# Loading queries and keys two tokens per lane: 512-byte runs, and the even and odd tokens of a tile kept apart

## The chip, the cores and the metric

The kernel runs on one core of a Trainium2 chip. The core has a matrix engine (PE, with its own weight loads, PEld), a vector engine (DVE), a scalar engine for activations (ACT), a general engine (POOL), and SP, which in this kernel only issues transfers. Sixteen DMA engines carry the transfers. The engines run apart from each other and meet at semaphores. The metric is the time of one execution on the device in microseconds (us), as a median of several; lower is better.

## The reference

Two layers are computed, one after the other. The first is attention with 4 batches, 8 heads, 768 tokens and 64 numbers per head. Each token sees the first 8 tokens ("global") and the 96 tokens up to itself ("local"), with a bias that falls linearly with distance:

```python
scores = scale * q @ k^T                                  # per batch and head
rel = pos[:, None] - pos[None, :]
is_global = pos[None, :] < 8
is_local = (rel >= 0) & (rel < 96)
dist = where(is_global & ~is_local, 96.0, abs(rel))
scores = where(is_global | is_local, scores - slope[h] * dist, -1e9)
x = softmax(scores) @ v                                   # heads side by side: 4 x 768 x 512
```

The global rule holds with no regard to order, so a token among the first 8 sees the others of the 8 that come after it.

The second layer is a mixture of 4 attention experts over `x`, each with a head of 64 numbers and causal, and the best 2 of 4 weighted by a gate:

```python
logits = x @ w_gate; the two largest per token, softmax over the two
for e in range(4):
    ye = softmax(causal(scale * (x @ wq[e]) @ (x @ wk[e])^T)) @ (x @ wv[e]) @ wo[e]
    out += weight_of_e_per_token * ye                     # out: 4 x 768 x 512
```

Inputs and output are float32. The kernel works in float16 between them and accumulates in float32.

## The kernel before, in words

**Units.** The work is cut into 24 units `u`: 4 batches times 6 tiles of 128 tokens (`ri` is the tile's number in its batch, `P` = 128). `unit(u)` writes down all operations of one unit. A unit has a front (the first layer) and a back (the second layer).

**Front.** Three loads (`ldq`, `ldk`, `ldv`, L519) bring 128 tokens of all 8 heads into `raw`, one token per lane, so that a lane receives 8 runs of 256 bytes (one head's 64 float32). POOL casts them to float16 (`cq`, `ck` into `qk16`, `cv` into `V1`). PE transposes queries and keys of a pair of heads at a time (`tq`, L536, 8 transposes per unit into one PSUM tile), and DVE copies the result to `qkT` (`eq`). PE makes the scores transposed, keys on lanes and queries along the row (`s0`, `s1`, L559: tile `sc`, one half of the heads each, with the tile's own keys and those of the tile before it). ACT takes the exponential (`x0`, `x1`, L563), DVE multiplies by a precomputed factor `M` that holds both bias and mask (`m0`, `m1`, L568; `M0` in the first tile of a batch), PE multiplies with the values (`z0`, `z1`, L576 and L579), whose column of ones gives the softmax sum, and DVE divides (`r0`, `n0` and so on, L590 and L592) into `x16`.

**Global tokens.** The 8 global keys and values of a batch are saved from its tile 0 (`kg`, `vg`, into `KG` and `VG`). When tile `u` has been used as own tile, they are written over the first 8 keys and values of it (`kp` on POOL, `vp` by a DMA on SP, L600), so that the next tile, which reads tile `u` as the tile before, meets the global tokens there. With a reach of 96 those 8 places are not otherwise seen by it.

**Back.** PE transposes `x16` (`tx`, L608), taking every fourth column so that the contraction index matches the weights' layout; DVE copies to `xT` (`ex`). PE projects to the queries and keys of the four experts (`pq`, L618, 16 matmuls) and to values and gate logits (`pv`, L624); the first is copied to `QK2` (`eqk`), the second to `V2` (`ev`). Scores of the second layer go against all earlier tiles of the batch (`s2`, L658), ACT takes exponentials (`x2`, L662), POOL clears the part above the diagonal (`af`, L670), PE multiplies with the values (`y2`, L682, up to 24 matmuls), DVE weights the result (`rz`, `cw`, `n2`), PE transposes (`tz`, L700) and projects (`po`, L705), ACT copies to `o_sb` (`eo`) and SP stores it (`so`, L714; 128 runs of 2 KB).

**Order of the work.** Every engine executes its instructions in the order in which the program gives them. That order is made while the program is built, by a small planner, `Stream`. Every operation is entered with the engines that may do it and an assumed length, with the operations it must follow, and with a rank. `Stream.run` repeatedly takes the operation with the earliest possible start by the assumed lengths (the key is start + `OTHER` if the second of two allowed engines does it + `ALPHA` * rank) and emits it. So the order is fixed on every engine, and the choice of engine for operations that have two (`eqk`, `ev`, `eo`, `m0`, `m1`, `kg`, `kp`) is made there too. SP is a queue like the others: a transfer that waits holds back all that come after it in the list. The program also has each transfer wait until the one eight places earlier in SP's list has landed, so that at most eight are under way.

**Buffers.** `R` = 4: `raw`, `qkT`, `V1` and most others are rings of four tiles, `qk16` of three. PSUM has two slots for scores (`s`) and four for the rest (`w`).

A `general_path` at the end is taken only if sums leave a safe range; it doesn't run here. One helper, `copy` (L358), does all casts and copies, so these are told apart by their tiles.

Of the kernel before, what the change touches and what calls it, by code (L numbers as in the profile page):

```python
# [16 lines left out]
P = 128  # L17
# [4 lines left out]
PACE, ALPHA, TURN = 6.00622, 0.000375979, 0.1  # L22
OTHER = {"m0": 3.12, "m1": 3.35, "eqk": 1.71, "ev": 14.02, "eo": 5.29, "kg": -15.22, "kp": 7.23}
RANK = {
    "ldq": 3.09, "ldk": -1.4103, "ldv": 10.549, "cq": 15.151, "ck": -10.082, "cv": -4.5336,
    "tq": -71.653, "eq": 55.538, "kg": 47.24, "vg": 107.76, "kp": -9.0259, "vp": -19.463,
    "s0": -7.8612, "s1": -17.799, "x0": -50.605, "x1": -67.881, "m0": 14.187, "m1": 99.879,
    "z0": -20.335, "z1": -37.532, "r0": -131.8, "r1": -26.257, "n0": 17.285, "n1": 25.757,
    "tx": -57.992, "ex": 9.4907, "pq": -14.609, "eqk": -26.055, "pv": 28.034, "ev": 73.988,
    "xr": 65.128, "mx": 2.1683, "wr": 21.14, "zi": 51.323, "s2": 11.269, "s2+": 19.618,  # L30
    "x2": 60.753, "x2+": 71.931, "af": -92.082, "y2": 41.953, "rz": 30.062, "cw": 42.106,
    "n2": -35.324, "tz": -7.6056, "ez": -136.19, "po": 59.119, "eo": 47.072, "so": -50.942,
}
W_RANK = -47.481, 2.337, 16.829, -53.198, 17.758
# [287 lines left out]
def kernel(  # L322
# [40 lines left out]
    R = 4  # L363
    ident = const.tile([P, P], FH, name="ident")
    w32 = const.tile([P, 3, E, nko, Hd], F32, name="w32")
# [6 lines left out]
    d = const.tile([P, 2 * P], F32, name="d")  # L372
    dg = const.tile([P, P], F32, name="dg")
# [6 lines left out]
    KG = ring(2, [P, H // 2, N_G], FH, "KG")  # L380
    VG = ring(2, [N_G, H, DV + 1], FH, "VG")
    raw = ring(R, [P, 3, H, Dh], F32, "raw")
    qk16 = ring(3, [P, 2, H, Dh], FH, "qk16")
    qkT = ring(R, [P, 2, H // 2, P], FH, "qkT")
# [22 lines left out]

    def c_iota(e):

        for n in range(2):  # L410
            pool.iota(di[:, n * P:(n + 1) * P], pattern=[[1, P]], channel_multiplier=-1, base=n * P)

    def c_mask(e):
        pool.affine_select(out=d[:, 0:P], in_=d[:, 0:P], pattern=[[1, P]], channel_multiplier=-1,
                           base=0, compare_op=Alu.is_ge, fill=HUGE)
        for n in range(2):
            t = d[:, n * P:(n + 1) * P]
            pool.affine_select(out=t, in_=t, pattern=[[-1, P]], channel_multiplier=1,
                               base=N_L - 1 - n * P, compare_op=Alu.is_ge, fill=HUGE)

    def c_dg(e):

        pool.memset(dg[:, :], float(N_L))
        pool.affine_select(out=dg[:, :], in_=dg[:, :], pattern=[[0, P]], channel_multiplier=-1,
                           base=N_G - 1, compare_op=Alu.is_ge, fill=HUGE)
# [21 lines left out]
    st.add("mask", c_mask, {"POOL": 0.9}, ["d"], rank=-18.0)  # L447
# [48 lines left out]
    def unit(u):  # L496
# [21 lines left out]
        def load(n, src):  # L518
            return lambda e: nc.sync.dma_start(raw[i][:, n, :, :],  # L519
                                               src[b, :, rows, :].rearrange("h s d -> s h d"))  # L520

        for n, src in enumerate((q, k, v)):
            add("ld" + "qkv"[n], load(n, src), {"DMA": 1.2}, [("c" + "qkv"[n], u - R)])
        for n in range(2):
            add("c" + "qk"[n], lambda e, n=n: copy(e, qk16[u % 3][:, n, :, :], raw[i][:, n, :, :]),
                {"POOL": 0.53} if u else ({"POOL": 0.53}, {"DVE": 0.4})[n],
                ["ld" + "qk"[n], ("tq", u - 3)])
# [266 lines left out]
```

## Time and profile before

| | |
|---|---|
| median of 3 runs | 158.49 us (158.09 to 159.02) |
| the profiled execution's own time | 157.58 us |
| its span, first to last instruction | 155.8 us |
| TensorE clock granted, mean over the span | 0.983 (1.00 until 148 us) |
| busy PE, DVE, ACT, POOL | 124.4, 126.7, 111.0, 72.0 us |
| first and last PE instruction | start at 10.44, end at 149.15 us |
| last ACT copy of the output | start at 149.23 us, 0.58 us |
| read from and written to HBM | 20.98 MB and 6.29 MB |

The profile tells of one execution. Busy time is the time in which an engine has an instruction in flight; PE's matmuls are pipelined, so one 128x128 matmul lasts 0.22 us by itself but 16 of `pq` in a row take about 0.9 to 1.0 us. A row of groups gives the line, the engine, the operation, the tiles (out<-in), the shapes and the count, then busy us and mean ns of one, then the idle time just before such instructions and what ended it. A row of waits gives who waited for whom: us in total, times, longest. A row of windows gives, for a stretch of time, the busy us of each engine (and the count of its instructions), the granted clock, the time of all transfer packets as a share of the 16 DMA engines' time (packets overlap, so it can exceed 1) and GB/s.

### The profile page before, as it was taken

What the parts mean: (1) busy time and instruction counts of PE and PEld (TensorE: products, weight loads), DVE (VectorE), ACT (ScalarE), POOL (GpSimd) and SP (SyncE); (2) the same over time, 40 slices, a digit from 0 to 9 for tenths busy, and PEclk for the clock granted to TensorE, in tenths of its full rate; (3) what the DMA queues carried; (4) which work ended last, traced back from release to release, by engine and by line L of the source; (5) the groups of instructions that cost most, each with busy time, mean ns of one, the idle gap of its engine ahead of it and who ended that gap; (6) DMA issues with size and microseconds to landing.
All of it is one profiled execution on the core that took longest, in us unless ns stands there. A gap on an engine that the chain in (4) does not pass through costs nothing.

```text
span 155.8 us, 5666 instructions
## 1 busy us (share of the span) xinstructions
PE 124.4 (80%) x2246; PEld 99.6 (64%) x2246; DVE 126.7 (81%) x438; ACT 111.0 (71%) x186; POOL 72.0 (46%) x132
## 2 busy tenths in 40 slices
PE   0027885959888988998899989999699999999820
PEld 0015774737777767985777876867588788777400
DVE  3228678987999999898899999999699999978710
ACT  4902457646867987889499968996478879999810
POOL 5037433636476655557938465654392321221000
PEclk9999999999999999999999999999999999999985
DMA  2999669899997999998997999995990221232550
GB/s 52 315 222 215 180 201 231 166 203 234 222 215 137 207 251 217 212 199 172 260 230 206 224 232 199 265 210 144 221 186 4 76 76 67 74 135 74 196 208 13
DMA packets 80687, 27.85 MB, mean 179 GB/s; under 512 B 75632, under 2 KB 77328, under 8 KB 80656
## 3 DMA queue, kind: packets, MB, share of 16 engines
q1 hardware_dynamic: 80656, 27.45, 77.7%
q8 instruction: 18, 0.29, 0.9%
q14 instruction: 13, 0.11, 0.3%
HBM read 20.98 MB, written 6.29 MB: 175 GB/s over the span
## 4 chain that ended last, share of the span: by engine, by line
PE 35%; DVE 21%; DMA 20%; POOL 6%; ACT 5%; issue 5%; SPq 4%; POOLq 0%; ACTq 0%; DVEq 0%
DMA raw<-in_q_dram 13%; DMA raw<-in_k_dram 7%; PE pq L618 6%; DVE A L568 5%; POOL qk L358 5%; PE tq L536 5%; PE po L705 4%; PE z L682 4%; PE s L658 4%; DVE qkT L358 4%; PE pv L624 3%; ACT A L563 3%; PE sc L559 3%; DVE QK L358 2%; DVE cw L689 2%
## 5 line engine op out<-in xcount | busy, mean ns | idle before, releaser
L563 ACT ACTIVATE A<-sc 128x1024 f16<-128x1024 f32 (+1 forms) x48 | 44.8, 962 | 16.0 <-PE sc L559 15.8
L662 ACT ACTIVATE A<-s 128x1024 f16<-128x1024 f32 (+1 forms) x48 | 44.0, 929 | 9.1 <-PE s L658 9.0
L358 POOL CAST qk<-raw 128x512 f16<-128x512 f32 x47 | 31.4, 671 | 31.2 <-DMA raw<-in_q_dram 19.2
L568 DVE TENSOR_TENSOR A<-A,M 128x1024 f16<-128x1024 f16 (+1 forms) x48 | 32.8, 690 | 1.6 <-ACT A L563 1.4
L536 PE MATMUL tq<-ident,qk 128*128 128x128 f16 x192 | 16.1, 231 | 16.3 <-POOL qk L358 15.8
L618 PE MATMUL pq<-xT,wqk 128*128 128x128 f16 x384 | 26.2, 223 | 0.9 <-DVE xT L358 0.7
L670 POOL TENSOR_SCALAR_AFFINE_SELECT A<-A 128x512 f16<-128x512 f16 x24 | 16.8, 699 | 18.8 <-ACT A L662 17.7
L618 PEld LDWEIGHTS <-wqk 128*128 128x128 f16 x384 | 23.1, 100 | 2.6 <-issue 0.9
L536 PEld LDWEIGHTS <-qk 128*128 128x128 f16 x192 | 12.2, 103 | 19.3 <-POOL qk L358 18.1
L358 POOL CAST V<-raw 128x512 f16<-128x512 f32 x24 | 16.2, 675 | 12.2 <-DMA raw<-in_v_dram 6.8
L358 DVE COPY qkT<-tq 128x1024 f16<-128x1024 f16 x24 | 16.3, 678 | 4.1 <-PE tq L536 3.9
L576 PE MATMUL z<-V,A 128*128 128x65 f16 x192 | 17.7, 198 | 2.3 <-POOL V L358 0.9
L592 DVE TENSOR_TENSOR x<-z,rall 128x256 f16<-128x256 f32 x48 | 19.2, 412 | 0.0
L358 DVE CAST QK<-pq 128x512 f16<-128x512 f32 x24 | 16.3, 680 | 1.6 <-PE pq L618 1.6
L658 PE MATMUL s<-QK 64*128 64x128 f16 x336 | 16.2, 218 | 1.3 <-DVE QK L358 1.1
L559 PE MATMUL sc<-qkT 64*128 64x128 f16 x192 | 15.2, 226 | 1.9 <-DVE qkT L358 1.0
L576 PEld LDWEIGHTS <-A 128*128 128x128 f16 x192 | 13.7, 100 | 3.8 <-DVE A L568 1.2
L358 ACT COPY o_sb<-po 128x512 f32<-128x512 f32 x24 | 14.4, 606 | 2.2 <-PE po L705 1.3
L579 PE MATMUL z<-V,A 128*128 128x65 f16 x160 | 14.9, 195 | 0.1
L624 PE MATMUL pv<-wvg,xT 128*128 128x264 f16 x96 | 14.8, 276 | 0.0
L559 PEld LDWEIGHTS <-qkT 64*128 64x128 f16 x352 | 10.9, 97 | 5.9 <-issue 2.8
L705 PE MATMUL po<-wo,zT 128*128 128x512 f16 x48 | 14.3, 380 | 0.3 <-DVE zT L358 0.2
(57 smaller groups left out, 197.9 us busy)
## 6 DMA issues: line engine op xcount, KB each, us to landing
raw<-in_k_dram SPq DMA_DIRECT2D x24, 256.0 KB
raw<-in_q_dram SPq DMA_DIRECT2D x24, 256.0 KB
raw<-in_v_dram SPq DMA_DIRECT2D x24, 256.0 KB
out_dram<-o_sb SPq DMA_DIRECT2D x24, 256.0 KB
w<-in_moe_wq_dram SPq DMA_DIRECT2D x1, 512.0 KB
w<-in_moe_wk_dram SPq DMA_DIRECT2D x1, 512.0 KB
w<-in_moe_wv_dram SPq DMA_DIRECT2D x1, 512.0 KB
wo<-in_moe_wo_dram SPq DMA_DIRECT2D x1, 512.0 KB
```

Of the source, the lines that this page charges most:

```text
L358: act.copy(o, i) if e == "ACT" else (dve if e == "DVE" else pool).tensor_copy(o, i)
L536: nc.tensor.transpose(ps[:, s, p, :], qk16[u % 3][:, s, 2 * p:2 * p + 2, :], ident[:, :])
L559: mm(sc[:, par, pr, prev * P:(prev + 1) * P], lhsT=kt, rhs=qkT[i][L, 0, p, :], start=True, stop=True)
L563: act.activation(A1[(2 * u + hf) % (2 * R)][:, :, :, 0:w], T.pop(("s", u, hf))[:, :, :, 0:w], func=Exp, scale=scale1)
L568: eng[e].tensor_tensor(a, a, M[:, hf, :, :, :] if ri else M0[:, hf, :, :, :], op=Alu.mult)
L576: mm(z[:, h % 4, :], lhsT=a[:, par, pr, 0:P], rhs=V1[i][:, h, 0:DV], start=True, stop=not ri)
L592: add(f"n{hf}", lambda e, hf=hf, r1=r1: dve.tensor_tensor(x16[i][:, 256 * hf:256 * hf + 256].rearrange("p (h d) -> p h d", d=Dh), T.pop((" ...
L618: mm(ps[:, j, :], lhsT=wqk[:, ko, j, :], rhs=xT[i][:, ko, :], start=(ko == 0), stop=(ko == nko - 1))
L624: mm(ps[:, :], lhsT=xT[i][:, ko, :], rhs=wvg[:, ko, :], start=(ko == 0), stop=(ko == nko - 1))
L658: mm(sc[:, par, n, :], lhsT=QK2[b % 2][L, ki, 2 + p2, :], rhs=QK2[b % 2][L, ri, p2, :], start=True, stop=True)
L662: act.activation(A2[i][:, :, 4 * ch:4 * ch + m, :], T.pop(("s2", u, ch))[:, :, 0:m, :], func=Exp, scale=scale2)
L705: mm(ps[:, :], lhsT=zT[i][:, p2, :], rhs=wo[:, p2, :], start=(p2 == 0), stop=(p2 == E // 2 - 1))
```

## The change

Queries and keys are loaded, cast and transposed in blocks of two tiles. In a block of 256 tokens lane `p` receives tokens `2p` and `2p+1`, which lie side by side in HBM, so a run is 512 bytes. The cast sorts a lane's two tokens apart (`p h j d -> p j h d`), the transposes are done for even tokens (`j` = 0) and odd tokens (`j` = 1) separately, and so within each tile of 128 the tokens stand as 64 even ones followed by 64 odd ones. The values are loaded in the same order, with two transfers of 64 lanes each (still runs of 256 bytes). The order is undone where `x` is transposed anyway: the transpose multiplies with a permuted identity, `perm`. The mask factors and the 8 global tokens (now 4 even and 4 odd ones, so two pieces of 4 lanes) follow the new order. The planner's constants, ranks and some assumed lengths are new as well; which engine does an operation, and its place in the order, follow from them.

```diff
-PACE, ALPHA, TURN = 6.00622, 0.000375979, 0.1
-OTHER = {"m0": 3.12, "m1": 3.35, "eqk": 1.71, "ev": 14.02, "eo": 5.29, "kg": -15.22, "kp": 7.23}
+PACE, ALPHA, TURN = 8.35723, 4.54359e-06, 0.1
+OTHER = {"m0": 8.31, "m1": 7.38, "eqk": -0.06, "ev": 16.85, "eo": 9.76, "kg": -28.92, "kp": 23.68}
 RANK = {
...
-W_RANK = -47.481, 2.337, 16.829, -53.198, 17.758
+W_RANK = -104.69, -69.793, 42.697, 5.1292, 57.145
...
-    raw = ring(R, [P, 3, H, Dh], F32, "raw")
-    qk16 = ring(3, [P, 2, H, Dh], FH, "qk16")
-    qkT = ring(R, [P, 2, H // 2, P], FH, "qkT")
+    RB = 3
+    rawqk = ring(RB, [P, 2, H, 2, Dh], F32, "rawqk")
+    rawv = ring(R, [P, H, Dh], F32, "rawv")
+    qk16 = ring(RB, [P, 2, 2, H, Dh], FH, "qk16")
+    qkT = ring(RB, [P, 2, H // 2, 2, P], FH, "qkT")
...
+    def c_perm(e):
+        pool.tensor_copy(perm[:, :].rearrange("c (p j) -> c p j", j=2),
+                         ident[:, :].rearrange("c (j p) -> c p j", j=2))
...
     def c_mask(e):
-        pool.affine_select(out=d[:, 0:P], in_=d[:, 0:P], pattern=[[1, P]], channel_multiplier=-1,
-                           base=0, compare_op=Alu.is_ge, fill=HUGE)
...
+        for op, lim in ((Alu.is_lt, 0.0), (Alu.is_gt, N_L - 0.5)):
+            dve.tensor_scalar(dout[:, :], d[:, :], lim, HUGE, op0=op, op1=Alu.mult)
+            dve.tensor_tensor(d[:, :], d[:, :], dout[:, :], op=Alu.max)
...
-        for n, src in enumerate((q, k, v)):
-            add("ld" + "qkv"[n], load(n, src), {"DMA": 1.2}, [("c" + "qkv"[n], u - R)])
-        for n in range(2):
-            add("c" + "qk"[n], lambda e, n=n: copy(e, qk16[u % 3][:, n, :, :], raw[i][:, n, :, :]),
...
+        u0, bl = u - u % 2, u // 2
+        if u == u0:
+            for n, src in enumerate((q, k)):
+                x = "qk"[n]
+                r, h16, tb = rawqk[bl % RB], qk16[bl % RB], qkT[bl % RB]
+                add("ld" + x, lambda e, r=r, n=n, src=src: nc.sync.dma_start(
+                    r[:, n, :, :, :].rearrange("p h j d -> p h (j d)"),
+                    src[b, :, ri * P:(ri + 2) * P, :].rearrange("h (p j) d -> p h (j d)", j=2)),
+                    {"DMA": 1.85}, [("c" + x, u - 2 * RB)])
+                add("c" + x, lambda e, r=r, h16=h16, n=n: copy(
+                    e, h16[:, n, :, :, :], r[:, n, :, :, :].rearrange("p h j d -> p j h d")),
+                    {"POOL": 1.05} if u else ({"ACT": 0.95}, {"DVE": 0.6})[n],
+                    ["ld" + x, ("t" + x, u - 2 * RB)])
+                def tq(e, n=n, x=x, h16=h16):
+                    T["t" + x, u] = ps = wtile([P, H // 2, 2, 2, HP], FH, "t" + x)
+                    for p in range(H // 2):
+                        for j in range(2):
+                            nc.tensor.transpose(ps[:, p, :, j, :], h16[:, n, j, 2 * p:2 * p + 2, :], ident[:, :])
...
+        def load_v(e):
+            for j in range(2):
+                nc.sync.dma_start(rawv[i][j * HP:(j + 1) * HP, :, :],
+                                  v[b, :, rows, :].rearrange("h (p j) d -> j p h d", j=2)[j])
...
-            add("vp", lambda e: nc.sync.dma_start(V1[i][0:N_G, :, :], VG[b % 2][:, :, :]), {"DMA": 0.1},
+            def vp(e):
+                for j in range(2):
+                    L = slice(j * HP, j * HP + NG2)
+                    nc.sync.dma_start(V1[i][L, :, :], VG[b % 2][L, :, :])
...
-                nc.tensor.transpose(ps[:, ko, :], xv[:, ko, :], ident[:, :])
+                nc.tensor.transpose(ps[:, ko, :], xv[:, ko, :], perm[:, :])
```

## The prediction, made before the changed kernel was run

> **What bounds the kernel now.** I read the busy row first, then the windows, then the groups and waits of the engine that is fullest where it matters, and the transfers last.
>
> ```profile
> PE 124.4 (80%) x2246; PEld 99.6 (64%) x2246; DVE 126.7 (81%) x438; ACT 111.0 (71%) x186; POOL 72.0 (46%) x132
> ...
> DMA  2999669899997999998997999995990221232550
> q1 hardware_dynamic: 80656, 27.45, 77.7%
> ```
>
> Over the whole span nobody is full. By stage it differs; the columns below are the stretch and its length, then busy us (instructions) of PE, PEld, DVE, ACT, POOL, the clock, DMA share, GB/s:
>
> ```profile
> 12.00:36.00 24.00, 18.54 (x276) 15.09 (x276) 19.21 (x58) 12.89 (x20) 12.12 (x22) 1.00 0.90 201
> 36.00:116.00 80.00, 72.63 (x1384) 59.19 (x1382) 74.88 (x247) 63.19 (x98) 49.18 (x85) 1.00 1.00 213
> 116.00:148.00 32.00, 31.25 (x574) 24.20 (x572) 28.45 (x118) 28.87 (x51) 7.11 (x13) 1.00 0.25 87
> 120.00:136.00 16.00, 15.87 (x322) 12.77 (x321) 15.10 (x58) 13.89 (x25) 3.51 (x7) 1.00 0.20 71
> ```
>
> Until 116 us, while inputs are loaded, the DMA engines are full (share 1.00) at only 213 GB/s, DVE is at 94% and PE at 91%. After the loads PE is at 98%. So two things hold up the first stage, transfers and DVE, and in the last nothing is left but PE's own work.
>
> I keep the books by PE, because it works from 10.44 to 149.15 us and the end follows it by a fixed tail (one copy, one store: 6.65 us). Of these 138.7 us it is busy 124.4, so 14.3 us are lost. The waits say to whom (who waited for whom: us in total, times, longest):
>
> ```profile
> POOL qk L358 <- DMA raw<-in_q_dram: 19.2, 16, 6.5
> ...
> PE tq L536 <- POOL qk L358: 15.8, 10, 10.4
> ...
> PE s L658 <- DVE QK L358: 1.1, 1, 1.1
> ...
> PE sc L559 <- DVE qkT L358: 1.0, 2, 0.8
> ```
>
> The first PE wait includes the start (10.4), so 15.8 - 10.4 = 5.4 us inside the run are waits for casts that themselves waited for transfers. The other 14.3 - 5.4 = 8.9 us are many small waits; those that the table of groups gives to DVE (before `pq` 0.7, `z` 0.7 and 0.5, `sc` 1.0 and 0.4, `s` 1.1, `tx` 0.6, `tz` 0.6, `tq` 0.3 and 0.2, `po` 0.2) add up to 6.3.
>
> **Part 1: loads of queries and keys.** 48 transfers of 1,024 packets of 256 bytes become 24 of 1,024 packets of 512 bytes: 49,152 packets become 24,576. In the trace's packet records a 256-byte packet lasts 20.4 ns (mean of 73,728), one of 1,024 bytes 53.9 and one of 2,048 bytes 94.9. No 512-byte packet is there. Bounds: 20.4 (size costs nothing) and 40.8 (no better than two). I take the straight line between the 256 and 1,024 rows, 20.4 + 33.5/3 = 31.6. Then 49,152 x 20.4 = 1,003 us of engine time become 777, so 226/16 = 14 us are saved (0 to 31) of the 77.7% x 155.8 = 121 us that all queue packets take. Share 1.00 in the load stage falls to about 0.87. The Trainium skill (DMA: Bandwidth & Descriptors, Specifications) puts the least size for line rate at 512 bytes, with read-modify-write below it. By that rule the 512-byte packet would run at the rate of the 2,048-byte rows, an estimate of 94.9/4 = 23.7 ns and a saving of 26 us. Both leave the transfers off the limit.
>
> Rings also get deeper: three blocks are six tiles, before four tiles raw and three cast. I therefore take the 5.4 us of PE waits as gone: **-5.4** (0 to -5.4). What is late next is POOL: a cast of a block has 1,024 numbers per lane, between 0.61 (median of the 512 row) and twice that, and delivers two tiles at once. 22 of these replace 47, so POOL's sum does not grow.
>
> **Part 2: values and global tokens.** 24 value loads become 48 of 64 lanes with the same packets; 20 `vp` copies of 8 lanes become 40 of 4. SP issues 24 fewer loads of q and k, 24 more of v and 20 more `vp`. A `vp` issue takes 0.65 us (median), so SP gets 20 x 0.65 = 13 us more issue work in 155, mostly in time in which it stood waiting for `o_sb` (22.9 us in one row of its waits) or for `z`. At most eight transfers are under way, and 6 instead of 5 per unit must pass: 8 places then cover 1.33 units instead of 1.6, about 8 us at 6 us per unit, against a landing time of 4 to 6.7 us on the chain. Behind a `vp` that waits for its `z` stand the loads of the following blocks. I cost it at nothing inside the run; the cover is the deeper ring, and without it a late load costs what it did before (part 1's 0). A rule speaks against it: SBUF — State Buffer ("Can I just issue two DMAs to hit both halves?") of the Trainium skill says 64 lanes reach half of the 16 ports, 196 GB/s measured, and that two halves do not add up. By that rule a tile's values take an estimated 262 KB/196 GB/s = 1.34 us, 24 of them 2.6 us more than at the 213 GB/s of the windows, still within the 14 saved. Four more `vg` copies of about 0.69 us go to POOL, which is idle half the time.
>
> **Part 3: which engine copies QK.** The built order shows what the diff alone does not: with the new constants 16 of the 24 `eqk` copies go from DVE to ACT. From the groups:
>
> ```profile
> L358 DVE CAST QK<-pq 128x512 f16<-128x512 f32 x24 | 16.3, 680 | 1.6 <-PE pq L618 1.6
> ...
> L358 ACT COPY o_sb<-po 128x512 f32<-128x512 f32 x24 | 14.4, 606 | 2.2 <-PE po L705 1.3
> ```
>
> DVE loses 16 x 0.68 = 10.9 us, ACT gains 16 x 0.606 = 9.7 (the same shape of copy). DVE comes to 126.7 - 10.9 + 1.7 (mask, below) + 0.3 (the first block's cast) = 117.8, ACT to 111.0 + 9.7 + 1.1 (first block's cast of q, like the 128x1024 weight cast, 1.07) = 121.8; PE stays at 124.4, as its 2,246 matmuls keep their shapes. All three are then about equal, and DVE has 9 us of slack it lacked. Of the 6.3 us that PE loses to DVE I take half: **-3.2** (0 to -6.3; 0 if ACT's queue delays the copies as much as DVE's did).
>
> **Part 4: the start.** Three POOL selects (0.29 + 0.55 us) become four DVE operations on 128x256 float32. The rows nearest are 0.29 (cast 128x256) and 0.32 (128x128, two inputs), so 1.2 to 2.1 us, 1.7 taken. That delays ACT's 16 factor exponentials (3.40 to 7.55 us) by about a microsecond, still before the first cast that ACT does. SP's new list begins wq, wk, q0, k0, each 512 KB, where before half of q0 and k0 sufficed. From 4 us on at the 312 GB/s of 4 to 8 us, k0 (2.1 MB, of which 0.24 by 4 us) lands at about 10; before, q0 landed at 9.72. So first scores come at 12.5 to 13 instead of 12.26. The first values stand tenth, behind 3.7 MB: 15 to 20 us at 312 to 213 GB/s, against a cast at 13.39 before. `z` of unit 0 (14.28 before) comes that late; PE, DVE and ACT have the fronts of units 1 to 3 to do meanwhile, which the new order places there. **+1.0** (0 to +4).
>
> **Part 5: the end.** Before, after the last `pq` (139.28) PE has 7.6 us of work from several units until the last `y2` ends (146.87). In the new order only `po`, `y2` of unit 22, 24 `s2`, `tz`, `po` and 24 `y2` remain: 0.43 + 0.60 + 0.83 + 0.25 + 0.43 + 0.91 = 3.5 us. Unit 23's three exponentials of 1.03 us stand between its `s2` and `y2` with only 0.7 us of other work for PE, and the PSUM ring for scores has two places, so the third group waits for the first exponential. PE idles about **+1.6** (0 to +2.5).
>
> The remaining edits (ring shapes, `perm` in place of `ident`, transposes writing two runs of 64, 4-lane `kg`/`kp` pieces) issue as many instructions of the same size as before on PE, DVE and POOL: 0; the `perm` copy, once on POOL before 10 us, is covered by POOL's idle 6.5 us there.
>
> **Sum.** -5.4 - 3.2 + 1.0 + 1.6 = -6.0 us. The profiled execution took 157.58 (span 155.8 and 1.8 around it), so 151.6; the median shown lies 0.9 above that execution, which would make 152.5. I say 152.0.
>
> **Rivals.**
>
> 1. *The transfers stay the limit.* If a 512-byte packet costs about 40 ns, or the eight places bind, part 1 gives 0 and the time is 152.0 + 5.4 = 157.4. For it: the share of 1.00 and landing times over 4 us. Against: 355 GB/s worth of rate at 2 KB (71 GB/s at share 0.20).
> 2. *Slower: ACT becomes the bound, in its queue.* QK copies on ACT stand behind exponentials of 1.03 us, and `s2` of the unit and all later tiles of the batch wait for them. From 12 to 148 us ACT was busy 105.0 of 136 (77%); with 10.8 more it has 115.8. If it again reaches only the 79% of the middle stage, 115.8/0.79 = 146.6, 10.6 us more than 136: about 168. It decides from 115.8/136 = 85% on: below that share the kernel gets slower. Against: 28.87 of 32 (90%) in the last stage, and its idle rows before are waits for `sc` (15.8) and `s` (9.0), that is for PE and what PE waited for.
> 3. *A dense run.* Without transfer waits the whole run is as full as 116 to 148 us: 124.4/0.977 = 127.3 instead of 138.7, so -11.4, with the +1.0 and +1.6: 157.58 - 8.8 = 148.8, down to 146.2 without these.
> 4. *The start costs its upper bound*, 4 instead of 1: 155.0.
>
> **How the numbers follow.** My forecast with its own range 149.5 to 154.5: 0.50. Rival 3: 0.19. Rival 4: 0.10. Rival 1: 0.10, of which I count half within 0.5% (about what a measurement of this kernel can tell from no change; 157.7 to 159.3). Rival 2: 0.11, all slower. Faster: 0.50 + 0.19 + 0.10 + 0.03 of rival 1 = 0.82; same 0.05; slower 0.11 + 0.02 = 0.13. The range reaches from rival 3's low end, 146.2, to 158.4, which takes in rival 1 and leaves out rival 2 and a little below: about 2 in 10 with the unknown costs.
>
> **What would show it.** Right: DMA share clearly below 1 in the middle with 512-byte packets of 24 to 32 ns; PE's waits for POOL's casts inside the run under 2 us; DVE near 118 and ACT near 122; PE's first-to-last stretch near 132 us with about 8 lost. Wrong: PE waiting for ACT's QK or for `x` more than 5 us, a middle stage with ACT under 85%, `z` waiting for values past 20 us, or more than 3 us of PE idle after the last `pq`.

## The result, and the profile after

The changed kernel takes 173.18 us (median of 4 runs, 171.87 to 175.16) against 158.75 for the kernel before (4 runs): a ratio of 1.0896, with a 95% interval of 1.0804 to 1.0989. It is 9% slower. The forecast was 152.0, with a range up to 158.4; the direction was wrong. The ratios leave out executions more than 1.5% above the fastest of their kernel, the profiled one below among them, but its mean clock of 0.938 is that of the other three (0.938 to 0.941).

The profiled execution of the changed kernel took 175.16 us with a span of 173.4, and all times below are its own. First its busy row, its slices and its transfers:

```profile
PE 132.7 (77%) x2246; PEld 105.1 (61%) x2246; DVE 124.4 (72%) x426; ACT 121.4 (70%) x203; POOL 69.9 (40%) x110
...
PEclk9999999995699999999969999799999999999955
DMA  3999973995539788958989489485201121311121
...
q1 hardware_dynamic: 56080, 27.45, 63.7%
```

The transfers became lighter, as meant: 56,080 packets instead of 80,656, and 63.7% of 173.4 us = 110.5 us per DMA engine instead of 121. Nothing became full instead: every engine's share fell. But PE is busy 8.3 us longer for the same 2,246 matmuls, and the clock row, which was flat until 148 us (the kernel before: `PEclk9999999999999999999999999999999999999985`), has dips. The windows of the same kernel (the stretch and its length; busy us and instructions of PE, PEld, DVE, ACT, POOL; clock, DMA share, GB/s):

```profile
12.00:36.00 24.00, 18.75 (x281) 16.05 (x281) 19.86 (x50) 14.96 (x23) 13.21 (x18) 1.00 0.98 213
36.00:116.00 80.00, 65.53 (x1096) 51.71 (x1095) 59.74 (x204) 54.96 (x90) 42.53 (x59) 0.91 0.81 194
116.00:148.00 32.00, 30.24 (x565) 24.02 (x564) 26.34 (x97) 29.79 (x49) 9.53 (x19) 1.00 0.25 75
36.00:40.00 4.00, 1.65 (x28) 0.97 (x27) 2.76 (x13) 2.84 (x4) 1.60 (x2) 0.91 0.97 177
40.00:44.00 4.00, 3.89 (x29) 2.31 (x30) 2.85 (x5) 1.27 (x3) 3.48 (x6) 0.50 0.73 188
```

The loss lies in the middle stage. There PE did 1,096 matmuls where it did 1,384 before, DVE fell from 94% to 75%, ACT from 79% to 69%, and the DMA engines from 1.00 to 0.81: all wait for each other. The last two lines show what follows a bad stretch: PE is busy 1.65 of 4 us, then it is full for 4 us at half clock and gets through 29 matmuls (four of them large ones, of 128x512), where the kernel before gets through 60 smaller ones in the same four microseconds. The half clock lasts 13.65 us in all in this stage (6.83 us from 39.3 on, 3.41 each from 87.1 and 107.5 on).

Who waited for whom (us in total, times, longest), first PE's rows:

```profile
PE tq L553 <- ACT qk L359: 9.7, 1, 9.7
PE z L717 <- POOL A L705: 3.2, 2, 2.5
PE tx L643 <- DVE x L622: 3.0, 4, 1.6
PE z L609 <- DMA V<-VG: 3.0, 4, 1.7
PE tk L553 <- POOL qk L359: 2.9, 2, 1.9
PE z L606 <- POOL V L359: 2.9, 2, 1.7
PE tz L735 <- DVE z L727: 2.3, 4, 1.0
```

The first row is the start. PE's waits for query and key casts inside the run fell from 5.4 us to 3.9 (the `tk` row and two small ones). In their place stand waits for values (`V`) and for the copied global values (`V<-VG`), 5.9 us together, which were 0.9, and 3.2 us for POOL's clearing above the diagonal (`A`, L705), which were nothing. SP's rows for the same kernel:

```profile
SPq L749 <- ACT o_sb L359: 24.5, 14, 4.8
SPq L633 <- PE z L609: 19.5, 9, 3.8
SPq L633 <- PE z L606: 6.7, 3, 2.5
```

SP stands 26.2 us at the head of its list with a copy of global values (L633) that waits for `z`; before, it was 13.3 + 6.2 = 19.5:

```profile
SPq L714 <- ACT o_sb L358: 22.9, 16, 4.6
SPq L600 <- PE z L579: 13.3, 10, 3.3
SPq L600 <- PE z L576: 6.2, 4, 2.0
```

In PE's books (first to last matmul of the real work): before 138.7 us, after 157.5. Of the 18.8 us more, 8.3 are busy time and 10.5 idle. The changed kernel with whole value loads and no copies (below) is busy 126.4 and has no half clock before its end; 132.7 - 126.4 = 6.3 agrees with 13.65 us at half speed, which loses 6.8.

### The profile page after: what moved, and what is told of

Same layout as the page of the kernel before. It is cut to its first block, busy times and chain, and to the rows that moved or that the text cites. A ratio compares the mean times of both kernels' runs of the same rounds, so it can differ in the third digit from the quotient of the medians.

```text
span 173.4 us, 5632 instructions
## 1 busy us (share of the span) xinstructions
PE 132.7 (77%) x2246; PEld 105.1 (61%) x2246; DVE 124.4 (72%) x426; ACT 121.4 (70%) x203; POOL 69.9 (40%) x110
## 2 busy tenths in 40 slices
DMA packets 56110, 27.84 MB, mean 161 GB/s; under 512 B 26480, under 2 KB 52752, under 8 KB 56080
## 3 DMA queue, kind: packets, MB, share of 16 engines
q1 hardware_dynamic: 56080, 27.45, 63.7%
## 5 line engine op out<-in xcount | busy, mean ns | idle before, releaser
L593 ACT ACTIVATE A<-sc 128x1024 f16<-128x1024 f32 (+1 forms) x48 | 45.0, 960 | 12.3 <-PE sc L589 11.7
L598 DVE TENSOR_TENSOR A<-A,M 128x1024 f16<-128x1024 f16 (+1 forms) x48 | 36.4, 761 | 3.3 <-ACT A L593 3.0
L359 POOL CAST qk<-rawqk 128x1024 f16<-128x1024 f32 x22 | 24.5, 1112 | 28.6 <-DMA rawqk<-in_q_dram 17.3
L653 PE MATMUL pq<-xT,wqk 128*128 128x128 f16 x384 | 27.3, 228 | 0.2 <-DVE xT L359 0.2
L705 POOL TENSOR_SCALAR_AFFINE_SELECT A<-A 128x512 f16<-128x512 f16 x24 | 17.4, 727 | 22.9 <-ACT A L697 22.2
L359 POOL CAST V<-rawv 128x512 f16<-128x512 f32 x24 | 16.0, 670 | 24.0 <-DMA rawv<-in_v_dram 11.7
L553 PEld LDWEIGHTS <-qk 128*128 128x128 f16 x192 | 13.7, 112 | 16.5 <-ACT qk L359 9.7
L606 PE MATMUL z<-V,A 128*128 128x65 f16 x192 | 18.1, 202 | 3.5 <-POOL V L359 2.9
L589 PE MATMUL sc<-qkT 64*128 64x128 f16 x288 | 18.4, 240 | 2.3 <-DVE qkT L359 1.8
L622 DVE TENSOR_TENSOR x<-z,rall 128x256 f16<-128x256 f32 x48 | 19.5, 413 | 0.3
L553 PE MATMUL tq<-ident,qk 128*128 128x128 f16 x96 | 9.4, 256 | 10.8 <-ACT qk L359 9.7
L609 PE MATMUL z<-V,A 128*128 128x65 f16 x160 | 15.2, 198 | 3.0 <-DMA V<-VG 3.0
L717 PE MATMUL z<-V,A 128*128 128x65 f16 x336 | 14.4, 194 | 3.7 <-POOL A L705 3.2
L606 PEld LDWEIGHTS <-A 128*128 128x128 f16 x192 | 14.3, 103 | 4.3 <-issue 1.9
L740 PE MATMUL po<-wo,zT 128*128 128x512 f16 x48 | 16.1, 421 | 0.5 <-DVE zT L359 0.4
L717 PEld LDWEIGHTS <-A 128*128 128x128 f16 x336 | 12.4, 98 | 5.4 <-POOL A L705 3.5
```

What stands on the lines that cost most here:

```text
L359: act.copy(o, i) if e == "ACT" else (dve if e == "DVE" else pool).tensor_copy(o, i)
L553: nc.tensor.transpose(ps[:, p, :, j, :], h16[:, n, j, 2 * p:2 * p + 2, :], ident[:, :])
L589: mm(sc[:, par, pr, prev * P:(prev + 1) * P], lhsT=qkt(u - prev, 1)[L, p, :], rhs=qkt(u, 0)[L, p, :], start=True, stop=True)
L593: act.activation(A1[(2 * u + hf) % (2 * R)][:, :, :, 0:w], T.pop(("s", u, hf))[:, :, :, 0:w], func=Exp, scale=scale1)
L598: eng[e].tensor_tensor(a, a, M[:, hf, :, :, :] if ri else M0[:, hf, :, :, :], op=Alu.mult)
L606: mm(z[:, h % 4, :], lhsT=a[:, par, pr, 0:P], rhs=V1[i][:, h, 0:DV], start=True, stop=not ri)
```

## The experiments

All ratios are to the kernel before on the same chip, with their 95% intervals. In the names, `j` is the half of a pair.

### Taking parts out of the changed kernel

The planner's new constants, put alone into the kernel before, and the old ones put back into the changed kernel:

```diff
# before, with the changed kernel's PACE, ALPHA, OTHER, RANK, W_RANK
-PACE, ALPHA, TURN = 6.00622, 0.000375979, 0.1
+PACE, ALPHA, TURN = 8.35723, 4.54359e-06, 0.1
...
```

> The kernel before, with the planner's constants (PACE, ALPHA, OTHER, RANK, W_RANK) of the changed kernel and nothing else. Theory O (the new constants make the bad order, above all 16 QK copies on ACT and loads issued in a poor sequence): 168 to 174 us. Theory S (the split transfers on SP and what waits behind them): 157 to 161, as before, give or take another order of equal quality. Theory B (blocks of two tiles arrive late and in lumps): 157 to 161.

> The changed kernel with the constants of the kernel before (ranks of tq and eq also for tk and ek). Theory O: 156 to 161 us. Theories S and B: 168 to 176, since the transfers and blocks stay as they are.

Measured: 1.0417 (1.0339 to 1.0494) for the first and 1.1007 (1.0889 to 1.1125) for the second. Each set of constants does better in its own kernel; exchanging them makes neither explanation nor cure. The first lies between the ranges given, the second in that of S and B: the old constants in the changed kernel give 174.88 us, so the slowness isn't the constants alone.

Next, the global values not copied, the values loaded whole in one transfer, and both:

```diff
 def vp(e):
-    for j in range(2):
-        L = slice(j * HP, j * HP + NG2)
-        nc.sync.dma_start(V1[i][L, :, :], VG[b % 2][L, :, :])
+    pass
```

```diff
 def load_v(e):
-    for j in range(2):
-        nc.sync.dma_start(rawv[i][j * HP:(j + 1) * HP, :, :],
-                          v[b, :, rows, :].rearrange("h (p j) d -> j p h d", j=2)[j])
+    nc.sync.dma_start(rawv[i][:, :, :], v[b, :, rows, :].rearrange("h s d -> s h d"))
```

> The changed kernel in the same order on all engines, but the 20 pairs of copies V<-VG on SP are left out, so the tiles after a batch's first do not see the global values. It takes 27 us of issue work and all waits for z off SP. Theory S: 158 to 163 us, loads issued up to 4 us earlier, TensorE's clock at 1.00 in the middle. Theories O and B: 171 to 173, less the 3 us that z waited for V<-VG, so 168 to 171.

> The changed kernel in the same order, but each tile of values is one transfer of 128 lanes in natural token order (the values then stand in another order than the keys, which changes the numbers and not the work). It takes 24 transfers and some 17 to 24 us of issue work off SP and gives back places among the eight under way. Theory S: 163 to 168 us. Theories O and B: 170 to 173.

> The changed kernel in the same order, with both cuts at once: the copies V<-VG are left out (tiles after the first do not see the global values) and each tile of values is one transfer of 128 lanes in natural order. Each cut alone gave about 10 us (162.4 and 163.3 against 173). Theory S1 (SP's issue work and what queues behind it is the whole loss, and adds up): 151 to 154 us, below the kernel before. Theory S2 (either cut frees SP enough; what is left is the order and the halved clock): 160 to 163 us, two spells of halved clock still there.

> The changed kernel in the same order, with only the first of each pair of copies V<-VG (the odd four global values are not passed on). It keeps every wait of SP for z and takes away 20 issues of 0.64 us, 13 us, and 20 of the places among the eight under way. If issue work counts: 165 to 169 us, half of what leaving out both gave. If the wait for z at the head of the queue counts: 171 to 173, no change.

Measured: without the copies 1.0311 (1.0251 to 1.037); with whole value loads 1.0324 (1.0241 to 1.0407); with both 1.0009 (0.997 to 1.0049); with only the first of each pair of copies 1.058 (1.0481 to 1.0679). Almost the whole loss goes with the two things that part 2 of the forecast priced at nothing.

From 1.0009, halving the value loads brings 1.0311, the first 20 copies 1.058, the second 20 copies 1.0896. Taken the other way round, the 40 copies bring only 1.0324 as long as the values come whole, and halving the loads then adds 5.7%: together the two cost more (8.9%) than each alone (3.0 and 3.2%). Each single cut lands in theory S's range, but the clock still halves in both (6.83 and 13.65 us); both cuts at once give 158.74 us, which neither S1 nor S2 expected, with no half clock before the end. When only the second copy of each pair is left out, SP's waits for `z` stay (25.9 us, 26.2 with both), yet half the cost of the copies goes: 168.09 us, in the range given for issue work.

### Putting the splits into the kernel before

The converse: the order of all work as before, only the value loads split into lanes 0 to 63 and 64 to 127, and the copy of 8 lanes into two of 4.

```diff
 def load_v(e):
+    for j in range(2):
+        nc.sync.dma_start(raw[i][j * 64:(j + 1) * 64, 2, :, :],
+                          v[b, :, ri * P + j * 64:ri * P + (j + 1) * 64, :].rearrange("h s d -> s h d"))
 def vp(e):
+    for j in range(2):
+        nc.sync.dma_start(V1[i][j * 4:(j + 1) * 4, :, :], VG[b % 2][j * 4:(j + 1) * 4, :, :])
```

> The kernel before, its order unchanged, with nothing but the splits: each tile of values in two transfers of 64 lanes and each V<-VG in two of 4 lanes, natural order, 256-byte runs. SP gets 44 more issues, about 28 us. Theory S1: 166 to 174 us, as slow as the changed kernel without its gains. If the splits hurt only together with the new order: 157 to 162.

Measured: 1.0842 (1.071 to 1.0973), 172.79 us. The splits alone, with no block, no permutation and no new order, reproduce the loss. Of its waits:

```profile
PE tq L541 <- POOL qk L358: 26.3, 14, 10.1
```

Without the start this is 16.2 us of PE waiting for casts of queries and keys, where it was 5.4: transfers that nobody touched come late. Its clock also halves, four times, for 17 us.

Is it the number of transfers, or their lanes? The value loads alone, once in two transfers of 4 heads each on all 128 lanes, once in two of 64 lanes:

```diff
+nc.sync.dma_start(raw[i][:, 2, 4 * j:4 * j + 4, :], v[b, 4 * j:4 * j + 4, rows, :]...)   # by heads
+nc.sync.dma_start(raw[i][j * 64:(j + 1) * 64, 2, :, :], v[b, :, ri * P + j * 64:..., :]...)  # by lanes
```

> The kernel before in its own order, each tile of values in two transfers of 128 lanes and 4 heads each; V<-VG stays one. The number of transfers grows by 24 as with two halves of 64 lanes. If the number counts (issue slots, the eight under way): 163 to 167 us, like the same count by lanes. If the 64 lanes count (issue 0.66 instead of 0.39 us, and the half transfer that lands no sooner than a whole one): 158 to 161.

> The kernel before in its own order, each tile of values in two transfers of 64 lanes; V<-VG stays one. Value halves and copies split together cost 14 us. By SP's issue work the halves are some 23 of 28 us of it: 166 to 170 us. If the copies at the head of the queue count as much: 163 to 166.

Measured: by heads 1.0004 (0.9963 to 1.0045), by lanes 1.0476 (1.0442 to 1.051). The number of transfers, their bytes and their packets are equal; the lanes alone cost 4.8%. The view of transfers has the queue's packets (number, MB, share of 16 engines) and each group of transfers (count, KB each, median us from issue to landing), first by heads:

```profile
q1 hardware_dynamic: 81040, 27.45, 76.3%
...
raw<-in_v_dram SPq DMA_DIRECT2D x48, 128.0 KB, 3.7
```

and by lanes:

```profile
q1 hardware_dynamic: 81040, 27.45, 78.0%
...
raw<-in_v_dram SPq DMA_DIRECT2D x48, 128.0 KB, 4.7
```

These two medians are over the 5 of 48 loads whose landing the view tells. With the landings of all 48, worked out from the semaphore updates in the traces, a half on 128 lanes lands 4.1 us after its issue and one on 64 lanes 4.5, nearly as late as a whole tile in the kernel before (4.75). PE's waits for casts, by heads and by lanes, are 5.2 and 7.9 us without the start:

```profile
PE tq L541 <- POOL qk L358: 15.6, 8, 10.4
...
PE tq L541 <- POOL qk L358: 18.4, 12, 10.5
```

In the packet records the 256-byte packets last 21.5 ns on average instead of 20.3, which over 73,728 of them is 89 us of engine time, or 5.6 us on each of 16 engines: near the 7.5 us (4.76% of 157.18) that the kernel lost. The shortest issue on SP also goes from 0.39 to 0.60 us, but the sums of issue time hardly differ (37.1 and 39.4 us), so the issues are hardly the price.

The copies of global values alone:

```diff
 def vp(e):
+    for j in range(2):
+        nc.sync.dma_start(V1[i][j * 4:(j + 1) * 4, :, :], VG[b % 2][j * 4:(j + 1) * 4, :, :])
```

> The kernel before with only the global values copied in two transfers of 4 lanes instead of one of 8; the value loads stay whole. Theory of a sum: splitting both cost 8.4%, splitting the value loads alone 4.8%, so this alone should cost about 3.6% (1.025 to 1.045, 161.5 to 164.5 us). Rival, the two splits feed each other: alone each 4-lane copy issues in the idle time of SP and this is 0.995 to 1.015.

Measured: 1.0306 (1.0192 to 1.0419). The sum holds within the intervals: 4.8 + 3.1 = 7.9% against 8.4% for both.

### What the blocks are worth without the splits

The changed kernel without copies and with whole value loads only equalled the kernel before, which still has its 20 copies. The fair base is the kernel before without them:

```diff
-add("vp", lambda e: nc.sync.dma_start(V1[i][0:N_G, :, :], VG[b % 2][:, :, :]), {"DMA": 0.1},
+add("vp", lambda e: None, {"DMA": 0.1},
```

> The kernel before, with the copies of the global values (V<-VG) left out, so the second tile and later ones of a batch miss them; all else keeps its place. It is the counterpart of the changed kernel without these copies and with whole value loads (1.0009 of the kernel before). Theory: these copies hold back loads on SP's list, some 13 us of issue and 13.3 us of waits, so without them the kernel before gains 2 to 4%, to 151.5 to 155; then the blocks with their new order do not gain but lose 2 to 4% on equal terms. Rival: the copies are hidden in the kernel before, 0.995 to 1.005; then the blocks and the new order together are worth nothing either way.

Measured: 0.9757 (0.9672 to 0.9841), 153.75 us. So on equal terms the blocks with their order go from 0.9757 to 1.0009: they lose 2.5% (some 4 us). The queue of this kernel, from its page (packets, MB, share), and its middle window:

```profile
q1 hardware_dynamic: 80336, 27.28, 78.8%
```

```profile
36.00:116.00 80.00, 74.36 (x1425) 61.15 (x1423) 77.30 (x255) 65.32 (x103) 49.28 (x85) 1.00 0.94 206
```

And the same two of the changed kernel without splits and copies:

```profile
q1 hardware_dynamic: 55376, 27.28, 67.5%
```

```profile
36.00:116.00 80.00, 73.99 (x1365) 59.73 (x1365) 70.43 (x250) 67.68 (x114) 45.05 (x66) 1.00 0.77 194
```

The transfers do get lighter by what was forecast: 78.8% of 151.9 us is 119.7 per engine, 67.5% of 156.9 is 105.9, so 13.8 us saved (forecast 14). DMA share falls from 0.94 to 0.77, DVE is relieved, and PE does fewer matmuls all the same. In the second kernel no wait of PE for a cast is left inside the run, but others have grown (its table of waits):

```profile
PE tx L639 <- DVE x L620: 2.5, 3, 1.4
PE tz L731 <- DVE z L723: 2.5, 5, 1.0
PE sc L587 <- DVE qkT L359: 2.5, 2, 1.7
PE s L689 <- ACT A L693: 0.9, 1, 0.9
```

All rows together: for POOL's casts and copies 2.1 us without the start became 0, for DVE 7.7 became 11.2, for ACT 0.9 became 2.5. PE is busy 126.4 instead of 123.6 and idle 2.8 us more.

The traces show where it is busy longer: in the transposes and scores (`tq`, `tk`, `sc`) of the start. One of their matmuls, or of `pq`, lasts about 310 ns there and 216 to 219 later, and that until 25.8 us instead of 19.7 (20.9 in the kernel before), 120 of them instead of 64. The windows give the clock as 1.00 in that stretch, but the trace's clock records only begin at these times. The kernel before with only the new constants shows the same, until 26.2 us, so it comes with their order. It isn't where the kernel falls behind: by 36 us it has done 312 matmuls against 299, by 116 us 1,673 against 1,720.

Two kernels keep the blocks but bring the keys back into natural order at the copy out of PSUM (`ek`, which then writes every second place), so that values and copies go in one transfer each as before; one with the new constants, one with the old:

```diff
-copy(e, tb[:, n, :, :, :], T.pop(("t" + x, u)).rearrange("l h a j p -> l h a (j p)"))
+copy(e, dst.rearrange("l s (p j) -> l s j p", j=2), src.rearrange("l h a j p -> l (h a) j p"))  # keys
...
+nc.sync.dma_start(rawv[i][:, :, :], v[b, :, rows, :].rearrange("h s d -> s h d"))
+add("vp", lambda e: nc.sync.dma_start(V1[i][0:N_G, :, :], VG[b % 2][:, :, :]), {"DMA": 0.1},
```

> The changed kernel with the keys put back in natural token order when DVE copies them out of PSUM (12 copies that write every second place), so that values are one transfer per tile and V<-VG one copy of 8 lanes, as in the kernel before; queries stay even then odd and are put right by perm. Queries and keys still come in 512-byte runs, the planner's constants are the changed ones. SP is spared 24 value transfers and 20 copies, about 34 us of issue work. Theory S1: 153 to 158 us. Theory S2: 160 to 164. If the 12 copies take 1.1 instead of 0.68 us, DVE gains 5 us of work, within its slack.

> The 512-byte blocks of queries and keys with keys put back in natural order (one value transfer per tile, one V<-VG of 8 lanes), as in the run with keys natural, but with the planner's constants of the kernel before. The new constants cost the kernel before 4%. Theory S1 with a bad order on top: 154 to 159 us, the 512-byte runs' gain showing at last. If the blocks of two tiles themselves hurt (casts and transposes come in lumps, values late at the start): 161 to 166, as with the new constants.

Measured: 1.0307 (1.0167 to 1.0446) and 1.0781 (1.0763 to 1.0799). DVE is busy 128.3 and 135.4 us there. In the first, PE waits only 0.9 us for POOL's casts inside the run, though SP still has 20 copies; but its waits for DVE are about 13 us (6.3 before). So 512-byte loads without any split gained nothing in these two orders either; whether another order of the work would free the gain stays open.

### Where the copies of global values stand

If SP's wait at the head of its list is what the copies cost, taking them off that list should help. First as an engine's copy, POOL or ACT as the planner chooses (13 and 7 of them), which also makes a new order:

```diff
-add("vp", lambda e: nc.sync.dma_start(V1[i][0:N_G, :, :], VG[b % 2][:, :, :]), {"DMA": 0.1},
+add("vp", lambda e: copy(e, V1[i][0:N_G, :, :], VG[b % 2][:, :, :]), {"POOL": 0.55, "ACT": 0.5},
```

> The kernel before with V<-VG copied by POOL (13 of 20) or ACT (7) instead of by a transfer on SP; the planner makes a new order for it. SP loses 13 us of issue work and all its waits for z, POOL gains 13 x 0.69 and ACT 7 x 0.5. If the head of SP's queue holds up the loads of the kernel before too: 150 to 156 us. If not, or if POOL's casts now wait for z in place of SP: 158 to 164.

Measured: 1.0239 (1.0201 to 1.0278), 160.7 us, as the second case had it. Then as transfers, but issued by POOL, in the changed kernel and in the one before:

```diff
-nc.sync.dma_start(V1[i][L, :, :], VG[b % 2][L, :, :])
+nc.gpsimd.dma_start(V1[i][L, :, :], VG[b % 2][L, :, :])
```

> The changed kernel with its 40 copies of global values issued by POOL instead of SP; order otherwise kept. Theory: what these copies cost is that SP waits at each pair for z and holds the loads behind it; POOL is busy 40%, so off SP's list they cost about what leaving them out left, 1.03 to 1.05 (162 to 165 us), and SP's waits for z (26 us) are gone. Rival: POOL now waits for z with the casts behind it, and each issue occupies POOL for about a microsecond: 1.08 to 1.13, with POOL's waits for z above 20 us.

> The kernel before with its 20 copies of global values issued by POOL instead of SP. Theory: loads no longer stand behind SP's waits for z (13.3 us), so the DMA engines are fed more evenly: 0.975 to 0.995 (153 to 156.5 us), a version faster than both. Rival: casts on POOL stand behind z instead, which costs PE as much or more: 1.00 to 1.04.

Measured: 1.2035 (1.191 to 1.2161) and 1.0922 (1.081 to 1.1033); both are slower than even the rivals had it, and not by their way. The waits of the second:

```profile
PE tq L536 <- POOL qk L358: 10.8, 2, 10.0
...
PE z L579 <- DMA V<-VG: 8.8, 7, 1.9
```

PE's waits for casts are gone but for the start and 0.8 us, so SP's wait did hold loads back, and the casts on POOL don't suffer from its issues (0.52 us each). But `z` now waits for the copies, which land 3.7 us after POOL's issue (median), where it was 2.3 from SP (worked out as above). In the first, the row of `z` at L609 is 22.6 us.

Last, two moves with every other list the same: SP's output stores issued by ACT, and each copy set two places later on SP's list.

```diff
-add("so", lambda e: nc.sync.dma_start(out[b, rows, :], o_sb[i][:, :]), {"DMA": 0.7}, ["eo"])
+add("so", lambda e: nc.scalar.dma_start(out[b, rows, :], o_sb[i][:, :]), {"DMA": 0.7}, ["eo"])
```

```diff
 # Stream.run, at the end of a step
+for h in [h for h in held if h[0] in after or h[1] == 0]:
+    held.remove(h)
+    h[2]("DMA")
+if key[0] == "vp":
+    held.append([key, 2, fn])
+    continue
 fn(e)
+if e == "DMA":
+    for h in held:
+        h[1] -= 1
```

> The kernel before with its 24 output stores issued by ACT, which makes nearly all of the o_sb copies, instead of SP; every engine's order is kept otherwise. Theory: SP's waits for o_sb (22.9 us) hold loads behind them like its waits for z do, and ACT (71% busy) has room for 24 issues of about 0.4 us: 0.97 to 0.99 (153.5 to 157 us), a version faster than both. Rival: the wait for o_sb holds back nothing that is needed soon, or ACT's exponentials now stand behind the issues: 0.995 to 1.03.

> The kernel before with each copy of global values moved two places later on SP's list, behind the two transfers that stood after it (or right ahead of the work that needs it, if that comes sooner); the lists of PE, DVE, ACT and POOL are the same. Theory: what the copies cost is the wait for z at the head of SP's list with loads behind it, so most of the 2.4% that leaving them out saved comes back: 0.975 to 0.99, with SP's waits for z (19.5 us) below 8 and no new wait of PE for V<-VG above 2 us. Rival: the copies cost by their issues and places on the list, not by the wait, or z of the next tile now waits for them: 0.995 to 1.03.

Measured: stores on ACT 1.0058 (1.0005 to 1.011); copies two places later 1.081 (1.0727 to 1.0893). Taking away the 22.9 us that SP waited for `o_sb` bought nothing; SP then waited 26.8 instead of 13.3 us at L600 for the last part of `z`. The other result is the clearest of the study. Its waits (lines stand 9 later in this file):

```profile
PE z L588 <- DMA V<-VG: 14.4, 11, 3.0
...
PE tq L545 <- POOL qk L367: 10.4, 1, 10.4
```

Two loads are let past each copy, and the casts are in time: the 5.4 us of PE's waits for them are gone. But `z` of the next tile waits 14.4 us for the late copies, PE's clock is halved for 13.65 us before the end and PE is busy 130.5 us instead of 124.4, and the kernel loses 8.1%. So the copy stands on the path of the run itself (`z` of a tile, the copy, `z` of the next tile), and the loads behind it are on it too. Whichever goes first on SP's list, the other pays. Of these 18, only the kernel before without its copies, which leaves work out, is faster than the kernel before; the values split by heads, the stores on ACT and the changed kernel with neither half loads nor copies equal it within 2%.

## Why the prediction was wrong

Set side by side, the runs make a ladder, each step against the kernel before on its own chip: before without copies 0.9757; with blocks and new order 1.0009 (+2.5); value loads in halves 1.0311 (+3.0); first copy 1.058 (+2.7); second copy 1.0896 (+3.2). Against the kernel before, which already has one copy (+2.4), the changed kernel's 9.0% are 2.5 for blocks and order and 8.9 - 2.4 = 6.5 for halved values and split copies: about 4 and 10 us of 158.5. By their intervals, each step is known to about one point. How the 6.5 divide depends on the way taken: 3.0 for the values and 3.5 for the copies on this one, 5.7 and 0.7 over whole values with both copies (1.0324). The forecast had -6.0 for blocks and order and nothing for the rest.

- **Part 2 failed, and it is half of the miss.** "I cost it at nothing inside the run" was wrong by 10 us. The working counted SP's issue time and found it idle long enough, and it counted bytes and packets and found them the same. Neither was the price. 64 lanes make packets slower and a half nearly as late as a whole (4.5 us, 4.1 for a half on 128 lanes). And idle time of SP is not free: SP waits there for `z` because the copy is next on the path, and a second issue of 0.6 us delays the second copy, the `z` behind it and the loads behind that. That the second copies cost 3% is measured; this way of it is read from the moved copies. "Behind a `vp` that waits for its `z` stand the loads" was in the text; that the next `z` stands behind the `vp` was not. The cover named, the deeper ring, was for queries and keys only.
- **The rule dismissed there.** The Trainium skill (SBUF — State Buffer, "Can I just issue two DMAs to hit both halves?") says two half-lane transfers serialize and only one over all lanes reaches all ports. The pair by heads and by lanes agrees with it in sign; no run here shows the ports. The estimate of 2.6 us made from its rate was set against 14 us of saved transfer time; measured in the kernel before, the halves cost 7.5 us.
- **Part 1: the transfers were sized right, the gain wasn't there.** Between the two kernels without copies and half loads, 13.8 us per engine were saved (forecast 14); in the changed kernel itself 10.6; the 512-byte packet lasts 34.3 ns on average in the changed kernel (median 27; forecast 31.6, and 23.7 by the rate of the skill's DMA: Bandwidth & Descriptors, Specifications, which no run bears out). And the blocks do take PE's waits for casts away: without half loads 1.9 us were left with 40 copies on SP, 0.9 with 20 (keys natural) and none without. The step that failed is to count these 5.4 us as time. Each of these kernels has other waits in their place, mostly for DVE, and is not faster than the kernel before. The waits also had a second cause: the kernel before, without its copies, has only 11.8 - 10.1 = 1.7 us of them left, so two thirds of them go with the loads held behind `vp`, which the wait table doesn't say:

```profile
PE tq L536 <- POOL qk L358: 11.8, 5, 10.1
```

- **Part 3: the move was right, its gain was not.** 16 copies went to ACT, as two groups show:

```profile
L359 ACT CAST QK<-pq 128x512 f16<-128x512 f32 x16 | 9.4, 589 | 6.7 <-PE pq L653 6.3
...
L359 DVE CAST QK<-pq 128x512 f16<-128x512 f32 x8 | 5.5, 691 | 7.7 <-PE pq L653 7.7
```

  ACT came to 121.4 (forecast 121.8), DVE to 124.4 (forecast 117.8), or 122.5 without splits and copies. Its 48 multiplications by the factor `M` took 36.4 us instead of 32.8 in the changed kernel, which the forecast held constant, and the cast of `wo` (0.7) was moved to it. And PE's waits for DVE rose instead of falling by 3.2: from 6.3 to 8.6 us in the changed kernel, from 7.7 to 11.2 between the two without copies, where DVE's sum fell from 127.4 to 122.5. So they don't follow DVE's sum; the long ones are for `n0`, `n2` and `eq`, and the new constants alone, in the kernel before, bring about 11 us of them.
- **The marks of part 4 and part 5 held.** First scores at 12.8 us (12.5 to 13), `z` of unit 0 at 19.2 (15 to 20). After the last `pq` PE is idle 2.6 us, 0.7 before: 1.9 more, forecast 1.6. What part 4 left out is that matmuls stay slow until 25.6 us instead of 20.9, which makes PE's work grow where "PE stays at 124.4" was written: it is 126.4 even without half loads and copies.
- **The rivals.** Rival 2 had the sign, not the cause: ACT in the middle stage is at 69%, below the 85% named, but because it starves (its longest waits are for PE, 11.7 us for `sc`, 9.3 for `po`); PE waits for ACT 2.1 us in all. Rival 1's "eight places bind" is refuted by the loads split by heads, which add 24 transfers at no cost in the kernel before; in the changed kernel all eight are under way for only 2.9 us, by the trace's issues and landings. No rival named the lanes, the copy's place on the path, or the clock. Of the signs of being wrong, ACT under 85% came true, though not for its reason; `z` of unit 0 was in time, but later ones did wait for values (2.9 us, at 37.1 and 53.5).
- **The clock** is a part of these steps: once waits bunch up, PE's clock halves and the same matmuls take longer, some 6 to 7 us in the changed kernel. Kernels with one split only, in the old order, show no such dip before the end; with both they do. In the new order one is enough (6.83 and 13.65 us). That the bunched waits set it off is read from their sequence in the traces; no run took the gaps away with all else kept.

## What to carry to other kernels

Before a transfer is cut in two, ask which lanes each half covers: halves over all lanes were free here, halves of the lanes cost 3 to 6%. A queue's idle time is not spare when its head waits for the critical chain; a small transfer there is priced by what stands behind it and by who needs it next, and moving it just shows the other side. And a wait table names the last link: before counting a wait as gain, take its supposed cause away alone and see whether the time follows.

## What was not expected of the hardware

- Twenty copies of 8 KB or 4 KB, 0.6% of the bytes or less, cost 2.4 to 3.2% of the time in four counts, 0.2 to 0.25 us each, and half of that in a fifth (40 copies 3.2%, with blocks and whole value loads).
- The clock fell to half for 3.41 or 6.83 us after stretches of 3.4 us in which PE was busy about half or less (0.48, 0.45 and 0.19 in the changed kernel), though its longest single gap was 2.52 us. The Trainium skill (TensorE: Matmul & The Clock Gate, "HAM oscillation — how this bites in real kernels") warns of idle gaps above about 3.4 us; here several shorter ones in a row were enough. The line is not sharp: 0.53 in the kernel before and 0.51 elsewhere in the changed one kept the clock, and in the changed kernel without copies it fell after 0.62. In each run the falls lie whole multiples of 3.41 us apart.
- 256, 512, 1,024 and 2,048 bytes last 18, 27, 46 and 84 ns (medians) per packet in the changed kernel: an offset of about 9 ns and a straight line, with no step at 512. The means are higher (20.9, 34.3, 56.4 and 88.3), and in other runs of the blocks the median of 512 bytes is 27 to 34.
